# Loading a kernel's mode weights in rows of 4 KB instead of 2 KB, with 64-row products in place of 128-row ones

## The chip, the cores and the metric

The kernel runs on one core of a Trainium2 chip. The metric is the device time of one execution in microseconds (us), the median of several runs. An engine's name stands for the unit that it drives: PE is the matrix unit (TensorE), PEld its weight loads, DVE the vector engine, ACT the scalar engine, POOL GpSimd, SP the sync engine, which only issues transfers here. A DMA is a transfer between the chip's main memory (HBM) and the on-chip memory (SBUF); 16 DMA engines carry all of a core's transfers. PSUM is the memory that PE writes its sums to, in banks of 2 KB per partition.

## What is computed

The first half is a linear attention per batch `b` and head `h` (8 x 8 of them, 576 positions, 64 numbers per head); its result, with the heads side by side, is `x` of 8 x 576 x 512. The second half mixes in frequency space:

```python
X = np.fft.rfft(x, axis=1)                      # along the 576 positions
Xr, Xi = np.real(X[:, :64]), np.imag(X[:, :64]) # 64 modes are kept
Yr = einsum('bmd,mde->bme', Xr, w_r) - einsum('bmd,mde->bme', Xi, w_i)
Yi = einsum('bmd,mde->bme', Xr, w_i) + einsum('bmd,mde->bme', Xi, w_r)
Y[:, :64] = Yr + 1j * Yi
u = x + np.fft.irfft(Y, n=576, axis=1)
out = u + np.maximum(u @ w_ch, 0.0)
```

Every mode `m` has two 512 x 512 matrices of its own, `w_r[m]` and `w_i[m]`, in float32. That is 2 x 64 x 512 x 512 x 4 bytes = 134 MB, and the profile counts 164 MB read from HBM in all. Each weight is used with only 8 batches.

## The kernel before

**Attention.** The Python loop over `n` runs 34 times. Stage `n` computes attention for one batch and two heads (in the first eight stages: two batches and one head), and overlaps four steps of neighbouring stages: the transposes of stage `n+1`, the features of stage `n`, the sums and quotients of stage `n-1`, and `x_mm` of stage `n-2`. `x_mm` (line 344) multiplies the finished part of `x` (`xs_all`) with cosine and sine columns (`CF4`), that is, it takes the Fourier transform of 128 columns of `x`, and puts the result into `XT`: 128 partitions hold 128 of the 512 columns `d`, and the free dimension holds real and imaginary parts, batches and the 64 modes.

**The mode products.** The contraction over the 512 values of `d` is cut in four quarters of 128, and the 64 modes into groups of 8. So there are 32 groups, k = 0 to 31. `weights(k)` (line 156) issues the DMAs of a group, `wr` and `wi`, on POOL's queue; they read float32 and write bf16. `mode_mm(k)` (line 390) makes the products: PE holds a 32-column piece of `XT` (real and imaginary parts of 8 batches and, beside them, zeros or the negated parts) and streams one mode's 512 columns of weights past it. Four such products lie side by side, at PSUM partitions 32j to 32j+31. `mode_sum(k)` adds the result to `Yacc` on DVE. Groups k = 0 to 7 (the first quarter) have a form of their own: their loads and products are already cut into two halves of 64 partitions (lines 166 and 403). Groups k = 8 to 31 have one DMA per tensor (line 162) and 16 products of 128 rows (line 416): 8 with `wr`, then 8 with `wi`.

Three buffers for each of `wr` and `wi` (`NW = 3`) let two groups' loads lie in the queue ahead of the group in use: the loads of group k+3 are issued when `mode_mm(k)` has freed its buffers.

**Order.** Under `manual_schedule` every engine runs its instructions in the order in which the Python code issues them. In the attention loop `mode_mm` is the last PE work of a stage, at most one group per stage, and 22 groups (k = 0 to 21) are done there; groups 8 to 21 fall to the stages n = 17 to 30. The last ten, k = 22 to 31, come in a tail after the loop. There each group is followed on PE by a share of the other work (`pieces`: transposes of `x`, `flip_x`, line 654, and products with `w_ch`, `times_w`, line 665; `reordered`, line 692; for k >= 24 transposes of the sums, line 805, and for every other one `by_batch`, lines 705 and 711). After k = 31 come the inverse transform and the output: lines 753 to 776 on PE, ACT and DVE, and the output DMAs on SP.

Of the kernel before, what the change touches and what calls it, by code (L numbers as in the profile page):

```python
# [21 lines left out]
NCH = 5  # L22
# [4 lines left out]
def kernel(  # L27
# [11 lines left out]
    nc = tc.nc  # L39
# [14 lines left out]
    xs_all = pers.tile([128, B_ * NCH, DMODEL], BF16, name="xs_all")  # L54
# [8 lines left out]
    CF4 = const.tile([128, NCH, 4, 64], BF16, name="CF4")  # L63
# [92 lines left out]
    def weights(k):  # L156
        g, gi = groups[k]
        wt = {}
        for ri, w in ((0, moe_w_r), (1, moe_w_i)):
            t = pw.tile([128, 8, DMODEL], BF16, name=f"w{'ri'[ri]}", tag=f"w{ri}")  # L160
            if gi >= 0:
                nc.gpsimd.dma_start(  # L162
                    t, w[8 * gi:8 * gi + 8, g * 128:(g + 1) * 128, :].rearrange("m p e -> p m e"))
            else:
                for x in range(2):
                    mx = 16 * (-1 - gi) + 8 * x
                    nc.gpsimd.dma_start(
                        t[64 * x:64 * x + 64],
                        w[mx:mx + 8, g * 64:(g + 1) * 64, :].rearrange("m p e -> p m e"))
            wt[ri] = t  # L170
        W[k] = wt
# [172 lines left out]
    def x_mm(st):  # L344
        psx = psum.tile([128, 2, 4, 64], F32, name="psx", tag="tx", bufs=1)
        XT = XTs[st["xt"]][:, 16:80, :].rearrange("p (x y b) m -> p x y b m", x=2, y=4)
        if "bs" in st:

            h = st["h"]
            for i, b in enumerate(st["bs"]):  # L350
                for c in range(NCH):
                    for x in range(2):
                        nc.tensor.matmul(
                            psx[64 * x:64 * x + 64, i, :, :],
                            lhsT=xs_all[:, b * NCH + c, h * 64:(h + 1) * 64],
                            rhs=CF4[:, c, :, :],
                            start=(c == 0), stop=(c == NCH - 1),
                        )
        else:
            g = st["g"]  # L360
            for c in range(NCH):
                nc.tensor.matmul(
                    psx[:, 0, :, :],
                    lhsT=xs_all[:, st["b"] * NCH + c, g * 128:(g + 1) * 128],
                    rhs=CF4[:, c, :, :],
                    start=(c == 0), stop=(c == NCH - 1),
                )
        for i, b in enumerate(st["bs"] if "bs" in st else (st["b"],)):
            nc.scalar.copy(
                XT[:, :, 0:2, b, :],  # L370
                psx[:, i, :, :].rearrange("d (x y) m -> d x y m", x=2),
            )
# [17 lines left out]
    def mode_mm(k, tag="yr"):  # L390
        g, gi = groups[k]
        XT = XTs[1 - g if k < 8 else g % 2]
        wt = W.pop(k)
        if gi < 0:
            psY = psum.tile([128, 2, DMODEL], F32, name="psY2", tag="pC", bufs=1)
            for par in range(2):
                for ri in range(2):
                    for j in range(4):
                        for x in range(2):
                            r = slice(64 * x, 64 * x + 64)  # L400
                            m = 16 * (-1 - gi) + 8 * x + 2 * j + par
                            c0 = (16, 0, 48, 32)[2 * ri + par]
                            nc.tensor.matmul(
                                psY[32 * j:32 * j + 32, x, :],
                                lhsT=XT[r, c0:c0 + 32, m],
                                rhs=wt[ri][r, 2 * j + par, :],
                                start=(par == 0 and ri == 0), stop=(par == 1 and ri == 1),
                            )
            return psY
        psY = psum.tile([128, DMODEL], F32, name="psY", tag=tag, bufs=1)  # L410
        for ri in range(2):
            for par in range(2):
                for j in range(4):
                    m = 8 * gi + 2 * j + par
                    c0 = (16, 0, 48, 32)[2 * ri + par]
                    nc.tensor.matmul(  # L416
                        psY[32 * j:32 * j + 32, :],
                        lhsT=XT[:, c0:c0 + 32, m],
                        rhs=wt[ri][:, 2 * j + par, :],
                        start=(par == 0 and ri == 0), stop=(par == 1 and ri == 1),  # L420
                    )
        return psY

    def mode_sum(k, psY, pb=None):
# [100 lines left out]
    psY = None  # L525
# [3 lines left out]
    with tc.manual_schedule():  # L529
# [18 lines left out]
        for t in qk2s[2]:  # L548
            nc.gpsimd.memset(t[:, :, 9, :], 0.0)
        load_qk(2)  # L550
        weights(0)
        k_in = 1
        transp(S[0], "q")
        transp(S[0], "k")
        for n in range(N + 2):
# [9 lines left out]
            if psY is not None:  # L565
                mode_sum(k_out, psY)
                psY = None
# [17 lines left out]
            while k_in < min(k_out + NW, 2 if n < 3 else 32):  # L585
                weights(k_in)
                k_in += 1
# [17 lines left out]
            if old:  # L605
                x_mm(old)
            e = n - (N + 2 - N_EARLY)
# [14 lines left out]
            if k_out < K_IN_ATTN and n >= after[k_out] + 2:  # L622
                psY = mode_mm(k_out)
# [161 lines left out]
    with tc.manual_schedule():  # L785
        plan = {22: 3, 23: 3, 24: 2, 25: 2, 26: 2, 27: 1, 28: 2, 29: 1, 30: 1, 31: 0}
        while k_out < 32:
            k = k_out
            gi = groups[k][1]
            while k_in < min(k_out + NW, 32):  # L790
                weights(k_in)
                k_in += 1
            if k == 31:
                add_xw(u0)
            yst = mode_sum(k, mode_mm(k, "T3"), pb)
            k_out += 1
            if yst is not None:
# [89 lines left out]
```

## Time and profile before

| | |
|---|---|
| runs | 456.17 us median of 3 (455.78 to 456.91) |
| profiled execution: span | 456.7 us (one core; its span is the time that the profile gives for it) |
| its mean granted PE clock | 0.883 |
| busy share of the span | PE 66%, DVE 64%, ACT 57%, POOL 44%, PEld 43% |
| read from HBM | 163.64 MB |
| moved by DMA, counted as written | 97.70 MB in 84417 packets, of which 77136 have under 2 KB |
| loads of groups 8 to 31 | 24 x 2 DMAs of 1024 KB (as written, bf16), landing 25.8 us (`wr`) and 29.4 us (`wi`) after issue |
| loads of groups 0 to 7 | 8 x 4 DMAs of 512 KB |

Bytes are counted as they are written to SBUF. A weight is read as four bytes and written as two, so a rate of 207 GB/s of weights is 414 GB/s read. The share of the DMA engines can go above 1, as the times of packets overlap. A line of the timeline gives the start in us, the duration from the first instruction's start to the last one's end, the engine, the line of the kernel, the operation, its output and inputs, and how many there are; in brackets is the time for which the engine sat idle before, and who ended it.

### The profile page before, as it was taken

To read this page: it belongs to the slowest core of one execution; us is meant where nothing else is said; L and a number is where in the kernel's file an instruction comes from. 1 tells how busy PE (TensorE), PEld (TensorE's weight loads), DVE (VectorE), ACT (ScalarE), POOL (GpSimd) and SP (SyncE) were. 2 spreads that over 40 slices of the span, in tenths; PEclk is the share of its full clock that TensorE was granted. 3 is DMA by queue.
4 is the path that set the end of the run, shared out by engine and by line. 5 is a ranking of instruction groups with operands and counts; after the bars stand their busy time and mean duration, and the time that the engine had idled before them with its cause. 6 is when DMAs were issued, how large, how long until landed. Compare 5 with 4: busy or idle time off the path is not lost.

```text
span 456.7 us, 11065 instructions
## 1 busy us (share of the span) xinstructions
PE 301.7 (66%) x4637; PEld 197.6 (43%) x4637; DVE 292.0 (64%) x418; ACT 261.8 (57%) x528; POOL 198.8 (44%) x251
## 2 busy tenths in 40 slices
PE   3476776833767677655555544755578878868993
PEld 2355565622555565544333432433344445433341
DVE  6578789844988779876666472776322273653873
ACT  4576887833686877865545452765334455644662
POOL 3956476445563256553435231443021212100993
PEclk9976899876886769998778595999999999998997
DMA  6999999999999999999999999999999999990697
GB/s 179 195 228 222 225 213 226 221 206 216 221 228 217 230 219 222 224 219 229 218 207 217 218 218 218 207 203 207 207 207 207 207 207 207 207 179 11 223 341 299
DMA packets 84417, 97.70 MB, mean 214 GB/s; under 512 B 3152, under 2 KB 77136, under 8 KB 84368
## 3 DMA queue, kind: packets, MB, share of 16 engines
q0 software_dynamic: 75728, 76.75, 101.1%
q1 hardware_dynamic: 8480, 20.19, 12.8%
q8 instruction: 36, 0.59, 0.5%
q14 instruction: 13, 0.11, 0.1%
q10 hardware_dynamic: 160, 0.07, 0.1%
HBM read 163.64 MB, written 9.44 MB: 379 GB/s over the span
## 4 chain that ended last, share of the span: by engine, by line
DMA 34%; issue 24%; DVE 17%; PE 11%; POOL 7%; ACT 3%; SPq 1%; DVEq 0%; POOLq 0%; ACTq 0%
DMA wi<-in_moe_w_i_dram 29%; DVE mkq L233 6%; DMA wr<-in_moe_w_r_dram 4%; DVE xs_all L336 2%; DVE nd L322 2%; DVE tB L315 2%; POOL vaug L270 2%; PE ptr L184 1%; PE psNB L305 1%; ACT AA L240 1%; PE kvz L286 1%; PE psB L753 1%; DVE of L776 1%; SPq L122 1%; POOL wr L162 1%
## 5 line engine op out<-in xcount | busy, mean ns | idle before, releaser
L270 POOL TENSOR_TENSOR vaug<-vn,ee 128x576 bf16<-128x576 f32 x64 | 72.7, 1155 | 63.3 <-ACT ee L255 50.2
L240 ACT ACTIVATE AA<-psT 128x1024 bf16<-128x1024 f32 x64 | 62.0, 1021 | 43.6 <-PE psT L208 43.1
L262 ACT ACTIVATE e<-mkq 64x4 f32<-64x4 f32 (+1 forms) x128 | 26.3, 206 | 61.5 <-DVE mkq L233 59.2
L244 ACT ACTIVATE AA<-psk 128x1024 bf16<-128x1024 f32 x64 | 61.4, 1010 | 0.0
L162 POOL DMA_DIRECT2D wr<-in_moe_w_r_dram x24 | 21.9, 912 | 86.6 <-PE psY L416 77.8
L416 PEld LDWEIGHTS <-XT 128*32 128x32 bf16 x384 | 17.1, 171 | 56.6 <-issue 46.4
L667 ACT CAST xw<-psW 128x1024 bf16<-128x1024 f32 x17 | 17.2, 1013 | 40.5 <-PE psW L665 34.6
L233 DVE TENSOR_REDUCE mkq<-psk 128x8 f32<-128x1024 f32 x32 | 38.8, 1213 | 0.7 <-PE psk L199 0.7
L233 DVE TENSOR_REDUCE mkq<-psq 128x8 f32<-128x1024 f32 x32 | 38.9, 1217 | 0.4 <-PE psq L199 0.4
L435 DVE TENSOR_TENSOR Yacc<-psY,Yacc 128x512 f32<-128x512 f32 x16 | 11.0, 689 | 42.5 <-PE psY L416 42.5
L416 PE MATMUL psY<-wi,XT 128*32 128x512 bf16 x192 | 18.0, 435 | 28.8 <-DMA wi<-in_moe_w_i_dram 28.8
L286 PE MATMUL kvz<-vaug,AA 64*128 64x65 bf16 x1152 | 29.2, 210 | 11.5 <-POOL vaug L275 9.8
L190 DVE COPY kT<-ptr 128x640 bf16<-128x640 bf16 x32 | 15.7, 492 | 32.5 <-PE ptr L184 32.5
L665 PE MATMUL psW<-wchb,sT 128*128 128x512 bf16 x136 | 33.5, 391 | 2.1 <-ACT xw L667 2.1
L315 DVE TENSOR_TENSOR tB<-psNB,e 128x650 f32<-128x650 f32 x32 | 26.7, 833 | 11.2 <-PE psNB L305 10.6
L305 PEld LDWEIGHTS <-AA 128*128 128x128 bf16 x640 | 29.0, 110 | 9.3 <-issue 8.9
L286 PEld LDWEIGHTS <-AA 64*128 64x128 bf16 x1152 | 25.1, 107 | 15.9 <-issue 11.8
L162 POOL DMA_DIRECT2D wi<-in_moe_w_i_dram x24 | 21.1, 880 | 23.8 <-PE psY L416 20.5
L322 DVE TENSOR_TENSOR nd<-psNA,tB 128x650 f32<-128x650 f32 x32 | 26.7, 835 | 4.1 <-DVE tB L315 0.5
L416 PE MATMUL psY<-wr,XT 128*32 128x512 bf16 x192 | 17.0, 424 | 18.0 <-DMA wr<-in_moe_w_r_dram 8.7
L336 DVE TENSOR_TENSOR xs_all<-nd,rden 128x640 bf16<-128x640 f32 x32 | 28.0, 874 | 1.1
L184 PE MATMUL ptr<-ident_b,k 128*128 128x128 bf16 x160 | 17.9, 257 | 14.8 <-DVE qT L190 12.6
(132 smaller groups left out, 705.4 us busy)
## 6 DMA issues: line engine op xcount, KB each, us to landing
wr<-in_moe_w_r_dram POOLq DMA_DIRECT2D x24, 1024.0 KB, 25.8
wi<-in_moe_w_i_dram POOLq DMA_DIRECT2D x24, 1024.0 KB, 29.4
wr<-in_moe_w_r_dram POOLq DMA_DIRECT2D x16, 512.0 KB, 15.9
wi<-in_moe_w_i_dram POOLq DMA_DIRECT2D x16, 512.0 KB, 19.6
out_dram<-of SPq DMA_DIRECT2D x16, 512.0 KB, 3.8
vn<-in_v_dram SPq DMA_DIRECT2D x24, 288.0 KB, 5.8
q<-in_q_dram POOLq DMA_DIRECT2D x12, 288.0 KB, 19.3
k<-in_k_dram POOLq DMA_DIRECT2D x12, 288.0 KB, 20.0
```

The source lines that it names most:

```text
L162: nc.gpsimd.dma_start(t, w[8 * gi:8 * gi + 8, g * 128:(g + 1) * 128, :].rearrange("m p e -> p m e"))
L233: nc.vector.tensor_reduce(out=o, in_=i, axis=AX.X, op=ALU.max, apply_absolute_value=True)
L240: nc.scalar.activation(AA[:, 0, ab, 0:1024].rearrange("f (x j p) -> f j x p", j=2, p=64), st["psT"].rearrange("f j (x p) -> f j x p", p=64 ...
L244: nc.scalar.activation(AA[:, 1, ab, 0:1024].rearrange("p (c j f) -> p j c f", c=4, j=2), st["psk"], ACT.Exp, scale=sc)
L270: nc.gpsimd.tensor_tensor(out=vaug[:, ab, :, 0:64], in0=st["v"], in1=ee[:, ab, :].unsqueeze(2).to_broadcast([128, 9, D_]), op=ALU.mult,)
L286: nc.tensor.matmul(kvz[:, hh, ab * 65:(ab + 1) * 65], lhsT=AA[r, 1, ab, 128 * j:128 * j + 128], rhs=vaug[r, ab, j, :], start=(j == 0), sto ...
L305: nc.tensor.matmul(p[:, hh, 65 * c:65 * c + 65], lhsT=AA[:, 0, ab, x:x + 128], rhs=kvzF[:, hh, ab * 65:(ab + 1) * 65], start=True, stop=True,)
L315: nc.vector.tensor_tensor(out=tB, in0=st["psNB"], in1=e2.unsqueeze(3).to_broadcast([128, 2, NCH, 65]), op=ALU.mult,)
L322: nc.vector.tensor_tensor(out=nd, in0=st["psNA"], in1=st["tB"], op=ALU.add)
L336: nc.vector.tensor_tensor(out=xo, in0=nd[:, :, :, 0:64], in1=rden.to_broadcast([128, 2, NCH, 64]), op=ALU.mult,)
L416: nc.tensor.matmul(psY[32 * j:32 * j + 32, :], lhsT=XT[:, c0:c0 + 32, m], rhs=wt[ri][:, 2 * j + par, :], start=(par == 0 and ri == 0), sto ...
L665: nc.tensor.matmul(ps[:, x, :], lhsT=sT[:, x, dc, :], rhs=wchb[:, dc, :], start=(dc == 0), stop=(dc == 3))
```

## The change

Groups 8 to 31 are loaded in another layout. Partition p of each half (64 partitions) takes two neighbouring rows of `w`, d = 2p and 2p+1 of the quarter, which lie behind one another in HBM: one row of 2 x 512 x 4 = 4096 bytes is read and 2048 written, where it was 2048 and 1024. The lower half of the partitions holds the group's first four modes, the upper half the other four. One DMA per tensor becomes two, each of 64 partitions x 4 modes x 1024 elements (128 x 8 x 512 before).

`XT` has to follow: its partitions 0 to 63 now hold the even or the odd `d` (chosen by `i`, in the free dimension) for the lower four modes of each group, and 64 to 127 those for the upper four. `x_mm` makes it with 20 products of 128 x 64 by 128 columns, where it had 5 of 128 x 128 by 256. `mode_mm` has 32 products of 64 rows per group where it had 16 of 128: twice over `i`, each with half of the contraction.

```diff
@@ weights
-                nc.gpsimd.dma_start(
-                    t, w[8 * gi:8 * gi + 8, g * 128:(g + 1) * 128, :].rearrange("m p e -> p m e"))
+                for x in range(2):
+                    mx = 8 * gi + 4 * x
+                    nc.gpsimd.dma_start(
+                        t[64 * x:64 * x + 64].rearrange("p (m i) e -> p m (i e)", i=2),
+                        w[mx:mx + 4, g * 128:(g + 1) * 128, :].rearrange(
+                            "m (p i) e -> p m (i e)", i=2))
@@ x_mm
-            for c in range(NCH):
-                nc.tensor.matmul(
-                    psx[:, 0, :, :],
-                    lhsT=xs_all[:, st["b"] * NCH + c, g * 128:(g + 1) * 128],
-                    rhs=CF4[:, c, :, :],
-                    start=(c == 0), stop=(c == NCH - 1),
-                )
+            for i in range(2):
+                for c in range(NCH):
+                    cf = CF4[:, c].rearrange("p y (q r) -> p (y q) r", r=4)
+                    for x in range(2):
+                        nc.tensor.matmul(
+                            psx[64 * x:64 * x + 64, 0, :, 32 * i:32 * i + 32],
+                            lhsT=xs_all[:, st["b"] * NCH + c, g * 128 + i:(g + 1) * 128:2],
+                            rhs=cf[:, x::2, :],
+                            start=(c == 0), stop=(c == NCH - 1),
+                        )
@@ mode_mm
-                for j in range(4):
-                    m = 8 * gi + 2 * j + par
-                    c0 = (16, 0, 48, 32)[2 * ri + par]
-                    nc.tensor.matmul(
-                        psY[32 * j:32 * j + 32, :],
-                        lhsT=XT[:, c0:c0 + 32, m],
-                        rhs=wt[ri][:, 2 * j + par, :],
-                        start=(par == 0 and ri == 0), stop=(par == 1 and ri == 1),
-                    )
+                for i in range(2):
+                    for j in (0, 2, 1, 3):
+                        r = slice(64 * (j // 2), 64 * (j // 2) + 64)
+                        m = 2 * (j % 2) + par
+                        c0 = (16, 0, 48, 32)[2 * ri + par]
+                        nc.tensor.matmul(
+                            psY[32 * j:32 * j + 32, :],
+                            lhsT=XT[r, c0:c0 + 32, 32 * i + 4 * gi + m],
+                            rhs=wt[ri][r, 2 * m + i, :],
+                            start=(ri == 0 and par == 0 and i == 0),
+                            stop=(ri == 1 and par == 1 and i == 1),
+                        )
```

## The prediction

> **What bounds the kernel now.** I read the forty slices of the page first.
>
> ```profile
> PEclk9976899876886769998778595999999999998997
> DMA  6999999999999999999999999999999999990697
> GB/s 179 195 228 222 225 213 226 221 206 216 221 228 217 230 219 222 224 219 229 218 207 217 218 218 218 207 203 207 207 207 207 207 207 207 207 179 11 223 341 299
> ```
>
> The DMA engines are full from the second slice to about 407 us, where the last weights run out. Wherever weights alone move, the rate is 207 GB/s (414 read), so a group of 4.19 MB costs 4.19 MB / 414 GB/s = 10.13 us. That looks like a kernel bound by its loads. The timeline of PE says that only a part of it is. In the attention stages PE stands waiting for `wi`, up to the last group done there, k = 21:
>
> ```profile
> 280.93 1.11 PE L416 MATMUL psY<-wi,XT 128*32 128x512 bf16 x8 [4.77 <-DMA wi<-in_moe_w_i_dram]
> ...
> 291.29 0.69 PE L416 MATMUL psY<-wi,XT 128*32 128x512 bf16 x8 [0.20 <-DMA wi<-in_moe_w_i_dram]
> ...
> 312.08 0.69 PE L416 MATMUL psY<-wi,XT 128*32 128x512 bf16 x8 [0.97 <-DMA wi<-in_moe_w_i_dram]
> ```
>
> The waits of PE between 165 and 335 us add up to 37.1 us for the two tensors:
>
> ```profile
> PE psY L416 <- DMA wi<-in_moe_w_i_dram: 28.4, 11, 5.2
> ...
> PE psY L416 <- DMA wr<-in_moe_w_r_dram: 8.7, 3, 4.1
> ```
>
> In the tail (k = 22 to 31) the picture turns. From 331 to 403 us no product waits for a DMA: PE goes from group to group with its own work between, and short waits for DVE and ACT. The loads only catch it at k = 30, for 1.16 us. The last `wi` was issued at 388.4 and landed 26.0 us later, at 414.4; PE came to it at 415.56.
>
> ```profile
> 331.07 0.69 PE L416 MATMUL psY<-wr,XT 128*32 128x512 bf16 x8 [0.67 <-ACT xw L388]
> 331.50 0.69 PE L416 MATMUL psY<-wi,XT 128*32 128x512 bf16 x8
> ...
> 402.78 0.69 PE L416 MATMUL psY<-wr,XT 128*32 128x512 bf16 x8 [0.78 <-DVE sT L657]
> 404.63 0.69 PE L416 MATMUL psY<-wi,XT 128*32 128x512 bf16 x8 [1.16 <-DMA wi<-in_moe_w_i_dram]
> ...
> 410.72 3.22 PE L665 MATMUL psW<-wchb,sT 128*128 128x512 bf16 x8
> ...
> 415.56 0.69 PE L416 MATMUL psY<-wr,XT 128*32 128x512 bf16 x8
> ```
>
> So a faster load is worth something up to 312 us, and after 331 us every added us of PE work is paid in full. The change gives the one and takes the other.
>
> **The loads.** Per group 1024 rows of 4 KB replace 2048 of 2 KB. No row of the trace has 4 KB reads with a cast, so the gain is bounded by rows next to it. The rows of q and k are read in 2304 bytes with the same cast, an eighth longer; around their landings (176.7 and 179.6 us) the rate is 208 in place of 207:
>
> ```profile
> 36.00:40.00 4.00, 1.88 (x54) 1.53 (x54) 3.52 (x7) 3.52 (x10) 1.19 (x3) 0.88 1.24 206
> 176.00:180.00 4.00, 3.01 (x57) 2.27 (x55) 3.46 (x6) 2.77 (x7) 3.87 (x6) 1.00 1.24 208
> 340.00:360.00 20.00, 16.60 (x132) 8.68 (x134) 5.26 (x8) 9.50 (x10) 3.50 (x4) 1.00 1.24 207
> ```
>
> (Window, its length, PE, PEld, DVE, ACT and POOL busy, PE clock, DMA share, GB/s.) If a row costs a fixed part and a part by bytes, 0.5% at an eighth longer means a fixed part of 0.5% / 0.111 = 4.5%, and rows twice as long save half of it: 2.25%, 0.23 us per group. With rounding it may be 0 to 1%, so 0 to 0.45 us per group; I take 0.23. The Trainium skill (DMA: Bandwidth & Descriptors, "Why small descriptors are slow (HBM only)") gives a packet 3 cycles beside its 32-byte beats; estimated from that, 2 x (64 + 3) = 134 cycles become 131, 2.2%, and the sum would be the same.
>
> Halves of 64 partitions cost nothing by the window 36 to 40 us: the first quarter's loads have that form and run at 206. POOL issues four DMAs per group instead of two. A 1024-row one takes 0.90 us, a 512-row one 0.71; in line with these a 256-row one would take 0.6, so 2.4 us instead of 1.8 per group. Behind it on POOL stands `vaug` (line 270), which waits 2 to 2.6 us for ACT in these stages anyway; if that cover were gone, 0.6 us per stage would go to a stage that waits 2.7 us for its weights on average.
>
> The gain starts at k = 11: k = 8 to 10 are loaded ahead and wait for their stages, and their buffers come free when PE gets there (170.7 us), as now. The queue is then just short of empty (share 1.18 instead of 1.20 for such a mix between 172 and 176 us), and buffers freed later than now cost it 0.4 us (the added `wr` products, below). So `wi` of k = 18 lands 8 x 0.23 - 0.4 = 1.4 us earlier, that of k = 21 2.1.
>
> **The products.** The trace has both forms.
>
> ```profile
> L416 PE MATMUL psY<-wi,XT 128*32 128x512 bf16 x192 | 18.0, 435 | 28.8 <-DMA wi<-in_moe_w_i_dram 28.8
> L403 PE MATMUL psY<-wr,XT 64*32 64x512 bf16 x128 | 7.9, 443 | 1.9 <-ACT XT L369 1.8
> ```
>
> ```profile
> 67.26 0.48 PE L403 MATMUL psY<-wr,XT 64*32 64x512 bf16 x8
> 67.47 0.48 PE L403 MATMUL psY<-wi,XT 64*32 64x512 bf16 x8
> ```
>
> Of the 128-row form 8 take 0.43 us, start to start (331.07 to 331.50): four lie side by side, two rounds of 0.215. Of the 64-row form 8 take 0.21 (67.26 to 67.47): eight lie side by side in one such round. A round is thus the passing of 512 columns, whatever the rows. The changed `mode_mm` uses only four places (two quarters of the columns in the lower rows, the other two in the upper), each eight times per group: 8 rounds where there are 4. That is 0.86 us more per group, 0.43 before `wi` and 0.43 behind its landing. Bounds: 0 (eight side by side) to 32 products one by one (last but one rival).
>
> **`x_mm`.** Five products of 256 columns take 0.63 us now; 20 of 128 columns, two side by side, are 10 passes of 0.053 = 0.53 us, and the nearest row with 64 columns of weights and 128 streamed (line 181) starts ten in 0.31, so 20 in 0.62. The other end is line 353, 20 of 256 columns in 1.2 us: 0.6 more. I take 0. Until n = 31 it has cover either way (DVE's 2.7 us of lines 315 to 336, or ACT); only in the last two stages would 0.6 each be seen.
>
> **The sum**, on the profiled execution (456.7 us). k = 18: `wi` at 280.93 - 1.4 = 279.5, its products 0.43 longer. k = 19: `wr` at 290.40 - 1.0 = 289.4, `wi` 0.86 behind it, at 290.3 (landing 289.6). k = 20: 299.4 and 300.3. k = 21: 309.2 and 310.0, which is also its landing: 2.1 earlier than 312.08. k = 22: 331.07 - 2.1 + 0.43 = 329.4. Eight groups (22 to 29) add 8 x 0.86 = 6.9: k = 30 at 408.0, `wi` at 408.9 without a wait, 4.2 later than 404.63. With the rest of its products +4.65, and k = 31 adds 0.86: +5.5, so 462.2 us. The loads (last one about 410) no longer matter there. The slow products at 410.72 (3.22 us at a clock of 0.52, where others take 1.9) are left as they are; without them it would be 1.4 less. The runs' median is 0.5 below this execution: **461.7 us**.
>
> **The rivals.**
> - *Rows of 4 KB are no faster*, per byte as now: k = 22 comes 0.8 later, the end 8.0: 464.2. For it speaks that 207 against 208 is within rounding.
> - *They are twice as good* (0.45 per group): k = 18 lands 3.2 earlier, but the stages from k = 19 on then bind themselves; k = 22 comes 3.45 earlier, the end is +3.75: 459.9. More speed of the loads hardly shows any more.
> - *Faster than before: the 64-row products overlap as at line 403.* If the extra rounds vanish in overlap, `mode_mm` costs what it costs now, k = 22 comes 2.1 earlier, k = 30 loses its wait, and the end comes 3.5 earlier: 452.7. It decides below some 0.3 us added per group. Against it: line 403 has eight places, this code four.
> - *Row halves shut each other out.* The order of j alternates lower and upper rows, and all write one PSUM bank; in line 403 the halves write two banks. If products of different halves can't run together, 32 x 0.213 = 6.8 us replace 1.7 of each group: 10 x 6 us in the tail and 14 x 6 less the 37 us of waits before, about 560 us. The Trainium skill (TensorEngine Tiling (Array Packing), "Gotcha 1: PSUM Pressure") says that different row tiles can't access one bank at the same time; by that rule this case would be the likely one, and no row here has it. Against it: the halves write different partitions.
> - *Loads in halves are slower.* The first ones ran at 173 to 185 GB/s between 18 and 22 us. At 180 a group would take 11.6 us, and 21 groups add 31 us: 488. Against it: 206 at 36 to 40 us and after.
>
> **How the numbers follow.** Forecast 0.66 (its own range 460 to 463.5: the slow clock, 0.1 us more or less per group); no gain of the loads 0.12; twice the gain 0.08; overlap 0.07; one bank 0.04; slow halves 0.03. What a measurement of this kernel can tell is about 0.3%, 1.4 us. Faster by more: 0.07 for the overlap and 0.01 for the unforeseen; within: 0.06, from parts of overlap and gain together; slower: 0.86. The range leaves out overlap, bank and slow halves: 457.5 to 466.
>
> **What would show it.** PE's `wr` and `wi` in the tail 0.86 us apart, twice 0.43; tail loads at 212 GB/s; `wi` of k = 21 started near 310, k = 22 near 329; no DMA wait at k = 30. Products 0.43 apart, or the tail's groups no longer spaced (the ten from 331 to 415 us) by 0.9 more, would make it wrong; so would waits for `wi` in the tail.

## The result, and the profile after

The changed kernel takes 475.36 us (median of 4 runs, 472.45 to 476.93) against 456.22 us (4 runs) on the same chip: a ratio of 1.040, 95% interval 1.036 to 1.044. It is slower, as forecast, but by 19 us and not by 5.5, and lies 9 us above the range. The profiled execution has a span of 474.2 us, where the working of the prediction ends at 462.2.

The slices of the page of after, to be laid beside the first fence of the prediction:

```profile
PEclk9985998867785888997979789998599999999998
DMA  6999999999999996999999999999999999950597
GB/s 178 192 228 227 217 227 218 218 217 217 214 225 210 231 173 126 231 221 220 221 217 225 211 231 222 211 211 211 204 162 189 184 201 205 211 110 1 188 345 298
DMA packets 60616, 97.80 MB, mean 206 GB/s; under 512 B 3921, under 2 KB 28753, under 8 KB 60561
```

Where weights alone move and nothing holds them up, the rate is now 211 GB/s, where it was 207, and the packets under 2 KB have fallen from 77136 to 28753: the rows are longer and move faster, as worked out. But there are holes that before does not have: 173 and 126 GB/s in slices 15 and 16 (166 to 190 us), and 162 to 205 from 344 us on. The second hole is harmless: there the loads wait for buffers that PE has not yet emptied. The first one is a loss in the middle of the loads. In windows of 4 us (columns as in the prediction's table of windows):

```profile
168.00:172.00 4.00, 2.27 (x56) 1.83 (x56) 2.86 (x6) 3.44 (x9) 3.18 (x5) 1.00 0.84 143
172.00:176.00 4.00, 2.50 (x56) 1.96 (x56) 3.22 (x6) 2.66 (x7) 0.61 (x1) 0.80 0.99 187
176.00:180.00 4.00, 3.58 (x56) 2.86 (x59) 2.88 (x5) 3.31 (x9) 2.46 (x3) 0.50 0.29 49
180.00:184.00 4.00, 3.74 (x75) 1.91 (x65) 2.98 (x4) 1.96 (x6) 2.37 (x4) 0.84 0.52 89
184.00:188.00 4.00, 2.77 (x85) 2.54 (x81) 3.30 (x8) 3.98 (x9) 2.77 (x5) 1.00 1.06 193
```

The mode products in the timeline of PE of after (the bracketed waits for DMA that before shows at these groups are gone):

```profile
179.38 1.93 PE L425 MATMUL psY<-wr,XT 64*32 64x512 bf16 x16
...
316.55 1.09 PE L425 MATMUL psY<-wr,XT 64*32 64x512 bf16 x16
317.47 1.03 PE L425 MATMUL psY<-wi,XT 64*32 64x512 bf16 x16
342.93 1.94 PE L425 MATMUL psY<-wr,XT 64*32 64x512 bf16 x16 [0.67 <-ACT xw L395]
...
421.48 1.09 PE L425 MATMUL psY<-wr,XT 64*32 64x512 bf16 x16 [0.78 <-DVE sT L667]
422.34 1.09 PE L425 MATMUL psY<-wi,XT 64*32 64x512 bf16 x16
...
432.33 1.09 PE L425 MATMUL psY<-wr,XT 64*32 64x512 bf16 x16
```

The tail is near the prediction. From k = 23 on `wr` and `wi` start 0.86 to 0.92 us apart, the wait for `wi` at k = 30 (422.34) is gone, and from k = 22 to k = 30 it takes 78.55 us, 6.84 more than the 71.71 of before; 6.9 was predicted (how much of that agreement is chance is said further down). What is wrong lies ahead of it: k = 22 starts at 342.93, not at 329.4. Group k = 8 is already late: it starts at 179.38, and at 170.72 in before. By the working of the prediction neither the longer rows nor the slower products count before k = 11.

The waits tell what PE stood for. The rows of after, by engine and line, with the total in us, how often, and the longest:

```profile
POOL wr L164 <- PE psY L425: 64.2, 9, 14.9
...
PE kvz L290 <- POOL vaug L279: 50.6, 17, 7.7
...
POOL wr L164 <- DMA wi<-in_moe_w_i_dram: 23.5, 12, 2.7
POOL wi L164 <- DMA wi<-in_moe_w_i_dram: 12.1, 7, 2.4
POOL wi L164 <- DMA k<-in_k_dram: 11.7, 5, 3.0
POOL wi L164 <- DMA wr<-in_moe_w_r_dram: 10.3, 6, 2.1
```

The same row of before is "PE kvz L286 <- POOL vaug L275: 9.8, 2, 6.1". `kvz` (`kv_mm`, line 290) is PE's first product with `vaug`, the scaled values that POOL makes (`vscale`, lines 274 and 279). So PE's 37 us of waits for weights have been exchanged for 51 us of waits for POOL (its waits for `wi` at line 425 are down to 3.7 us), and POOL itself stands before its *DMA issues*, waiting for the landing of other DMAs. All rows of line 164 that a DMA ended add up to 67.7 us in 39 waits; the loads of groups 8 to 31 in before (line 162) have one such wait, of 3.1 us.

POOL's own timeline of after shows by which rule it waits:

```profile
110.13 0.76 POOL L143 DMA_DIRECT2D q<-in_q_dram  x1 [0.19 <-issue]
111.77 0.70 POOL L143 DMA_DIRECT2D k<-in_k_dram  x1 [0.88 <-DMA wr<-in_moe_w_r_dram]
115.16 0.64 POOL L164 DMA_DIRECT2D wr<-in_moe_w_r_dram  x1 [2.68 <-DMA wi<-in_moe_w_i_dram]
118.20 0.61 POOL L164 DMA_DIRECT2D wr<-in_moe_w_r_dram  x1 [2.40 <-DMA wi<-in_moe_w_i_dram]
120.54 0.61 POOL L164 DMA_DIRECT2D wi<-in_moe_w_i_dram  x1 [1.73 <-PE psk L203]
122.84 0.61 POOL L164 DMA_DIRECT2D wi<-in_moe_w_i_dram  x1 [1.69 <-DMA wr<-in_moe_w_r_dram]
123.47 2.27 POOL L274 TENSOR_TENSOR vaug<-vn,ee 128x576 bf16<-128x576 f32 x2
125.68 0.26 POOL L279 CAST vaug<-ee 128x18 bf16<-128x18 f32 x1
125.81 0.66 POOL L164 DMA_DIRECT2D wr<-in_moe_w_r_dram  x1
127.94 0.61 POOL L164 DMA_DIRECT2D wr<-in_moe_w_r_dram  x1 [1.47 <-DMA wi<-in_moe_w_i_dram]
129.63 0.61 POOL L164 DMA_DIRECT2D wi<-in_moe_w_i_dram  x1 [1.07 <-DMA q<-in_q_dram]
132.87 0.61 POOL L164 DMA_DIRECT2D wi<-in_moe_w_i_dram  x1 [2.63 <-DMA k<-in_k_dram]
```

Count the DMAs. The `wi` at 129.63 waited for a `q`: the `q` of 110.13 is the eighth DMA before it. The `wi` at 132.87 waited for `k`: the `k` of 111.77 is the eighth before. The records of the DMAs in the traces name the semaphore that each one signals: in both kernels POOL's DMAs take eight of them in turn (110 to 117), and in neither does a DMA of POOL start before the eighth before it has landed. So no more than eight of POOL's DMAs are on their way, whatever their size, and the ninth holds POOL, with all that stands behind it in POOL's order. With two DMAs per group, three groups in flight make six, and a `q` and a `k` fill the eight. With four per group, three groups make twelve. From then on POOL issues at the rate of landings, 2 to 3 us apart; the four issues of a stage take 8 to 10 us with their waits, and `vaug`, which comes behind them, is late:

```profile
147.69 0.61 POOL L164 DMA_DIRECT2D wi<-in_moe_w_i_dram  x1 [1.63 <-DMA wr<-in_moe_w_r_dram]
148.32 2.27 POOL L274 TENSOR_TENSOR vaug<-vn,ee 128x576 bf16<-128x576 f32 x2
```

```profile
150.83 1.17 PE L290 MATMUL kvz<-vaug,AA 64*128 64x65 bf16 x36 [7.73 <-POOL vaug L279]
```

The first of these is POOL's, the second PE's timeline of after. PE stands for 7.7 us here for a load that has nothing to do with its stage. The same product in PE's timeline of before:

```profile
141.32 1.10 PE L286 MATMUL kvz<-vaug,AA 64*128 64x65 bf16 x36
```

There POOL issued the stage's two loads at 131.27 and 132.36 and started this `vaug` at 135.26, and PE did not wait for it. After is 9.5 us behind at this point, and 8.7 are left when k = 8 starts.

The hole at 168 to 188 us follows from that: all three buffers are full until k = 8 frees one.

### The profile page after: what moved, and what is told of

The parts are those of the page before. It is cut to its first block, busy times and chain, and to the rows that moved or that the text cites. A ratio compares the mean times of both kernels' runs of the same rounds, so it can differ in the third digit from the quotient of the medians.

```text
span 474.2 us, 12581 instructions
## 1 busy us (share of the span) xinstructions
PE 322.7 (68%) x5362; PEld 218.9 (46%) x5381; DVE 294.0 (62%) x418; ACT 262.3 (55%) x528; POOL 214.4 (45%) x299
## 2 busy tenths in 40 slices
DMA packets 60616, 97.80 MB, mean 206 GB/s; under 512 B 3921, under 2 KB 28753, under 8 KB 60561
## 4 chain that ended last, share of the span: by engine, by line
PE 29%; DMA 29%; DVE 13%; ACT 9%; POOL 9%; issue 8%; SPq 1%; DVEq 0%; ACTq 0%; POOLq 0%
DMA wi<-in_moe_w_i_dram 16%; DMA q<-in_q_dram 7%; PE psW L675 6%; PE psY L425 6%; DMA wr<-in_moe_w_r_dram 5%; POOL vaug L274 4%; DVE mkq L237 3%; ACT AA L244 2%; DVE nd L326 2%; DVE xs_all L340 2%; POOL wi L164 2%; PE kvz L290 2%; ACT AA L248 2%; PE psx L369 2%; PE pt L664 1%
## 5 line engine op out<-in xcount | busy, mean ns | idle before, releaser
L164 POOL DMA_DIRECT2D wr<-in_moe_w_r_dram x48 | 30.1, 630 | 96.9 <-PE psY L425 64.2
L290 PE MATMUL kvz<-vaug,AA 64*128 64x65 bf16 x1152 | 28.6, 208 | 51.4 <-POOL vaug L279 50.6
L164 POOL DMA_DIRECT2D wi<-in_moe_w_i_dram x48 | 29.6, 624 | 56.3 <-DMA wi<-in_moe_w_i_dram 12.1
L290 PEld LDWEIGHTS <-AA 64*128 64x128 bf16 x1152 | 25.7, 105 | 55.4 <-issue 50.6
L425 PEld LDWEIGHTS <-XT 64*32 64x32 bf16 x768 | 31.2, 138 | 28.6 <-issue 20.8
L299 ACT CAST kvzF<-kvz 128x260 bf16<-128x260 f32 x32 | 12.1, 379 | 44.3 <-PE kvz L290 44.1
L425 PE MATMUL psY<-wr,XT 64*32 64x512 bf16 x384 | 28.7, 418 | 8.2 <-ACT AA L252 4.1
L309 PEld LDWEIGHTS <-AA 128*128 128x128 bf16 x640 | 30.3, 112 | 6.8 <-issue 6.3
L675 PE MATMUL psW<-wchb,sT 128*128 128x512 bf16 x126 | 31.3, 379 | 2.6 <-ACT xw L677 2.1
L425 PE MATMUL psY<-wi,XT 64*32 64x512 bf16 x384 | 27.3, 381 | 3.7 <-DMA wi<-in_moe_w_i_dram 3.7
```

Source lines behind the costliest of these rows:

```text
L164: nc.gpsimd.dma_start(t[64 * x:64 * x + 64].rearrange("p (m i) e -> p m (i e)", i=2), w[mx:mx + 4, g * 128:(g + 1) * 128, :].rearrange("m ...
L290: nc.tensor.matmul(kvz[:, hh, ab * 65:(ab + 1) * 65], lhsT=AA[r, 1, ab, 128 * j:128 * j + 128], rhs=vaug[r, ab, j, :], start=(j == 0), sto ...
L309: nc.tensor.matmul(p[:, hh, 65 * c:65 * c + 65], lhsT=AA[:, 0, ab, x:x + 128], rhs=kvzF[:, hh, ab * 65:(ab + 1) * 65], start=True, stop=True,)
L425: nc.tensor.matmul(psY[32 * j:32 * j + 32, :], lhsT=XT[r, c0:c0 + 32, 32 * i + 4 * gi + m], rhs=wt[ri][r, 2 * m + i, :], start=(ri == 0 an ...
L675: nc.tensor.matmul(ps[:, x, :], lhsT=sT[:, x, dc, :], rhs=wchb[:, dc, :], start=(dc == 0), stop=(dc == 3))
```

## The experiments

Theory Q: the number of POOL's DMAs in flight. Rival P: the slower products themselves delay the attention stages. Rival H: transfers to halves of the partitions are slower. Each run is compared with the kernel before on the same chip: 456.20 us (13 runs) for the first four, 456.16 us (8 runs) for the next four, 457.10 us (17 runs) for the last. In the table, "k = 22" is the start of that group's first product in the profiled execution, "tail" the time from there to the first product of k = 31, "kvz" PE's wait there for `vaug`.

| kernel | median us | ratio [95%] | span | k = 22 | tail | kvz |
|---|---|---|---|---|---|---|
| before | 456.2 | 1 | 456.7 | 331.07 | 84.5 | 9.8 |
| after | 475.36 | 1.040 [1.036, 1.044] | 474.2 | 342.93 | 89.4 | 50.6 |
| e1_split_only | 467.61 | 1.027 [1.024, 1.029] | 467.0 | 344.24 | 81.7 | 48.1 |
| e2_products_twice | 466.21 | 1.022 [1.018, 1.027] | 461.3 | 330.78 | 88.7 | 9.9 |
| e3_rows_only | 453.37 | 0.993 [0.991, 0.996] | 452.7 | 329.94 | 81.7 | 10.7 |
| e4_after_vaug_first | 471.61 | 1.035 [1.030, 1.040] | 471.0 | 340.77 | 88.4 | 7.4 |
| e6_after_one_dma | 463.91 | 1.019 [1.015, 1.023] | 459.1 | 328.88 | 88.4 | 10.4 |
| e7_split_by_modes | 470.34 | 1.031 [1.026, 1.035] | 466.9 | 343.24 | 82.6 | 47.8 |
| e5_before_vaug_first | 463.52 | 1.015 [1.011, 1.020] | 463.3 | 337.82 | 84.4 | 4.0 |
| e8_after_two_ahead | 477.24 | 1.045 [1.040, 1.049] | 477.2 | 346.98 | 88.4 | 3.8 |
| e9_parts_in_halves | 455.51 | 0.996 [0.994, 0.998] | 455.0 | 332.31 | 81.8 | 8.4 |

### Only the number of DMAs: e1_split_only

```diff
@@ before, weights
-                nc.gpsimd.dma_start(
-                    t, w[8 * gi:8 * gi + 8, g * 128:(g + 1) * 128, :].rearrange("m p e -> p m e"))
+                for x in range(2):
+                    d0 = g * 128 + 64 * x
+                    nc.gpsimd.dma_start(
+                        t[64 * x:64 * x + 64],
+                        w[8 * gi:8 * gi + 8, d0:d0 + 64, :].rearrange("m p e -> p m e"))
```

> The kernel before, with each load of groups 8 to 31 cut into two DMAs of 64 partitions; rows stay 2 KB, products and layout as before. Theory Q (queue): the program gives POOL's DMAs eight semaphores in turn, so the ninth DMA outstanding waits, on POOL, for the first to land; with four DMAs per group instead of two POOL stands still, vaug behind it comes late and so does PE. Then this kernel shows most of the surprise: k = 22 starts 9 to 14 us later than the 331 us of before, total 465 to 470 us, and PE waits 40 us or more for vaug (9.8 before). Rival P (products): the delay in the attention stages comes from the 64-row products and the new x_mm; then this kernel is within 2 us of 456. Rival H (halves): 64-partition transfers are slower; then the rate in the tail is below 200 GB/s instead of 207.

467.61 us. Products, rows and `x_mm` are those of before, and yet k = 8 starts at 180.60 and k = 22 at 344.24, even a little later than in after. The waits of PE and of POOL in e1_split_only:

```profile
PE kvz L289 <- POOL vaug L278: 48.1, 14, 9.0
```

```profile
POOL wi L164 <- DMA wr<-in_moe_w_r_dram: 17.0, 9, 2.2
POOL wi L164 <- DMA wi<-in_moe_w_i_dram: 14.8, 7, 3.1
POOL wr L164 <- DMA wi<-in_moe_w_i_dram: 14.7, 9, 2.4
```

That is the picture of after. The rate between 320 and 330 us is 206 GB/s, where before has 207, so halves of 64 partitions are not slow: H falls. The delay comes without the slower products, so P is not needed for it. Q stands. The extra issue time alone is too small: an issue takes 0.70 us here, so four of them take 1.0 us more per group than the two of before, and single waits of `kvz` reach 9.0 us.

### Only the products: e2_products_twice

The products of `mode_mm` (k from 8 on) are made twice and both added, 32 of 128 rows in place of 16, in 8 rounds as in after (the mode part of the output is doubled). The loads are those of before.

```diff
@@ before, mode_mm
-            for par in range(2):
-                for j in range(4):
+            for rep in range(2):
+                for par in range(2):
+                    for j in range(4):
...
-                        start=(par == 0 and ri == 0), stop=(par == 1 and ri == 1),
+                            start=(rep == 0 and par == 0 and ri == 0),
+                            stop=(rep == 1 and par == 1 and ri == 1),
```

> The kernel before, with all mode products of groups 8 to 31 made and added twice (16 more products per group, four side by side, so 0.86 us more per group as in the changed kernel; the mode part of the output is doubled). Loads as before. Theory Q: the attention stages hardly move (k = 22 at 331 to 332.5), the ten groups of the tail add about 7 us, total 461 to 465. Rival P: the attention stages lose 10 us or more here too, total 470 or above.

466.21 us, 1.2 us above what was expected, with a profiled execution at the low end of its runs (463.12 us, span 461.3). In that one, k = 22 stands where it stood (330.78), `kvz` waits 9.9 us, and the tail takes 88.7 us in place of 84.5. The tail of before contains the wait at k = 30 and the slow products at 410.72; the tails of e1 and e3 have neither and take 81.7 us, so the products cost the tail 7.0 us. They cost the attention nothing in this execution; P falls for the attention as far as it shows. The other three runs are 2.5 to 4.4 us slower, and no profile of them says where.

### Only the rows: e3_rows_only

One DMA per tensor as in before, 128 partitions with rows of 4 KB. The partitions then hold 256 rows of four modes and not 128 of eight, so the products multiply other weights than the reference's; their shapes and number are those of before.

```diff
@@ before, weights
-                    t, w[8 * gi:8 * gi + 8, g * 128:(g + 1) * 128, :].rearrange("m p e -> p m e"))
+                    t.rearrange("p (m i) e -> p m (i e)", i=2),
+                    w[8 * gi:8 * gi + 4, (g - 1) * 128:(g + 1) * 128, :].rearrange(
+                        "m (p i) e -> p m (i e)", i=2))
```

> The kernel before, with each load of groups 8 to 31 still one DMA of 128 partitions but in 512 rows of 4 KB (four modes of 256 rows; the products get other weights than they should). Products as before. Theory Q and the prediction: 212 GB/s in place of 207, k = 22 2 us earlier, the end 2 to 3.5 us earlier: 452.5 to 454.5. If the gain of 4 KB rows in the changed kernel was an artefact of its emptier queue, 207 GB/s and 456.

453.37 us, 0.66% faster, span 452.7. The prediction's "overlap" rival gave a median of 452.7 for faster loads without slower products. The rate is 212 GB/s.

### After, with vaug ahead of the loads: e4_after_vaug_first

```diff
@@ after, the loop over n
-            if n < 4:
+            if cur:
                 vscale(cur)
...
-            if cur and n >= 4:
-                vscale(cur)
```

> The changed kernel, with the making of vaug put ahead of the weights' loads on POOL's queue in every stage. Theory Q: PE's wait for vaug goes from 50.6 to under 15 us and most of the surprise comes back: 462 to 467 us. If the waits for the queue hurt by starving the loads and not through vaug, or if P holds, it stays at 473 to 477.

471.61 us, only 4 us back, where 8 to 13 were expected. The wait of `kvz` is gone as wanted (7.4 us). But the loads now stand behind `vaug`, and `vaug` behind ACT; the first line is from the waits of POOL, the second from the page of e4:

```profile
POOL vaug L274 <- ACT ee L259: 66.2, 19, 6.3
```

```profile
GB/s 180 195 229 215 221 121 220 217 218 217 218 220 222 224 228 136 216 221 221 221 223 220 223 220 221 212 212 211 210 211 212 204 201 207 210 114 1 189 346 301
```

There are two holes. In the first (121 GB/s, 59 to 71 us) a `wr` that after issues at 60.51 is issued at 69.14, behind a `vaug` that waits 4.1 us for ACT. In the second (136 GB/s, 177 to 188 us) k = 8 is still late (177.52), and the loads that it makes room for then stand behind another wait for ACT, of 4.3 us. So it is not the order alone. As I read it, with eight places of half the size POOL has to be at hand at every landing, and it can't be while it also waits for ACT; no run separates that from the late start of k = 8. My expectation had left it out.

### Before, with vaug ahead: e5_before_vaug_first

The same edit in the kernel before, as a control.

> The kernel before with vaug ahead of the weight loads on POOL in every stage, the control to the same edit of after (which gave back some 4 of 19 us and moved the hold from vaug to the loads, whose issue then stood behind vaug's wait for ACT). Theory Q: with two DMAs per group there is little to gain (kvz waits 9.8 us for vaug in all) and the loads come up to 3 us later per group, though the depth of three groups covers that: 454 to 460, vaug's wait of kvz 2 to 8 us. A theory by which the order on POOL is the whole cost of the change would have a gain here of the 10 us that kvz waits: 446 to 450.

463.52 us, 7 us slower; both expectations missed. With two DMAs per group the loads first, `vaug` second is the better order by these 7 us. The timeline of PE, ACT and POOL shows why a late load feeds itself (the fences are one for each engine):

```profile
210.26 1.10 PE L416 MATMUL psY<-wi,XT 128*32 128x512 bf16 x8 [5.18 <-DMA wi<-in_moe_w_i_dram]
211.69 0.64 PE L208 MATMUL psT<-qT,w 64*128 64x512 bf16 x2
```

```profile
212.43 1.94 ACT L240 ACTIVATE AA<-psT 128x1024 bf16<-128x1024 f32 x2 [6.03 <-PE psT L208]
214.92 0.21 ACT L255 ACTIVATE ee<-mkq 128x9 f32<-128x9 f32 x1
```

```profile
215.22 2.27 POOL L270 TENSOR_TENSOR vaug<-vn,ee 128x576 bf16<-128x576 f32 x2 [8.54 <-ACT ee L255]
217.43 0.25 POOL L275 CAST vaug<-ee 128x18 bf16<-128x18 f32 x1
217.57 0.94 POOL L162 DMA_DIRECT2D wr<-in_moe_w_r_dram  x1
```

PE waits 5.2 us for a `wi`; the stage's `psT` stands behind it on PE, ACT behind `psT`, `vaug` behind ACT, and the next load behind `vaug`: it is issued at 217.57, 7 us after the products that freed a buffer began.

### After, with one DMA per tensor: e6_after_one_dma

Everything of after but the count of DMAs: `x_mm` with 20 products, 32 products of 64 rows per group, rows of 4 KB, and one DMA of 128 partitions per tensor as in e3 (so the weights are again other ones than the reference's).

```diff
@@ after, weights
-                for x in range(2):
-                    mx = 8 * gi + 4 * x
-                    nc.gpsimd.dma_start(
-                        t[64 * x:64 * x + 64].rearrange("p (m i) e -> p m (i e)", i=2),
-                        w[mx:mx + 4, g * 128:(g + 1) * 128, :].rearrange(
-                            "m (p i) e -> p m (i e)", i=2))
+                nc.gpsimd.dma_start(
+                    t.rearrange("p (m i) e -> p m (i e)", i=2),
+                    w[8 * gi:8 * gi + 4, (g - 1) * 128:(g + 1) * 128, :].rearrange(
+                        "m (p i) e -> p m (i e)", i=2))
```

> The kernel after with its two DMAs per tensor and group made one again: 128 partitions, four modes, 4 KB rows, the same 1 MB (the partitions then hold 256 rows of four modes, not 128 rows of eight, so the products multiply other weights; their number, order and shapes are those of after). So the 4 KB rows, the 64-row products and the new x_mm stay; only the number of DMAs goes back to two per group. Theory Q (POOL's DMAs take turns at eight places, and four per group do not fit): the delay in attention goes, k = 22 back at 329 to 332, PE's waits of kvz for vaug back to 9 to 15 us, no dip of the rate at 176 to 188, the tail stays that of after or of the doubled products (86 to 90 us), in all 458 to 466. Rival P (the slower products themselves delay attention): 470 to 476. Rival H (halves of 64 partitions are slow to move): it would also predict a gain, but the kernel that only split the loads moved its halves at 206 GB/s against 207, so H has little left.

463.91 us, where 461.7 was predicted for after. PE's timeline in e6 has k = 22 at the predicted place (329.4):

```profile
328.88 1.09 PE L423 MATMUL psY<-wr,XT 64*32 64x512 bf16 x16 [0.67 <-ACT xw L393]
329.74 1.09 PE L423 MATMUL psY<-wi,XT 64*32 64x512 bf16 x16
```

and PE's waits for `vaug` are back at the size of before:

```profile
PE kvz L288 <- POOL vaug L277: 10.4, 3, 6.4
```

The loss of after now splits in two, by medians: 463.91 - 456.16 = 7.8 us for rows, products and `x_mm` together, and 475.36 - 463.91 = 11.4 us for two DMAs more per group. The second part alone, in e1, was 467.61 - 456.20 = 11.4 us. That the two agree so closely is partly chance: the four runs of e6 lie between 460.93 and 466.69, and by the profiled executions alone the split is 2.4 and 15.1 us.

### The other cut: e7_split_by_modes

```diff
@@ before, weights
-                nc.gpsimd.dma_start(
-                    t, w[8 * gi:8 * gi + 8, g * 128:(g + 1) * 128, :].rearrange("m p e -> p m e"))
+                for x in range(2):
+                    mx = 8 * gi + 4 * x
+                    nc.gpsimd.dma_start(
+                        t[:, 4 * x:4 * x + 4, :],
+                        w[mx:mx + 4, g * 128:(g + 1) * 128, :].rearrange("m p e -> p m e"))
```

> The kernel before, with each weight load of k from 8 on cut in two by modes: two DMAs of 128 partitions, four modes each, 2 KB rows (the other cut, by partitions, took 467.6). Theory Q: it is the number of DMAs that counts, not which partitions they go to: 464 to 470, k = 22 at 341 to 347, waits of kvz for vaug 40 to 55 us. Rival H (halves of 64 partitions, or the two transfers' sharing of ports): as before, 455 to 458, waits of kvz for vaug at 10 us.

470.34 us and 47.8 us of `kvz` waits, with all 128 partitions in every DMA. It is the count, not the halves. The loss is 14.2 us, where e1 lost 11.4; why this cut costs 2.8 us more stays open.

### Fewer ahead: e8_after_two_ahead

```diff
@@ after
-    NW = 3
+    NW = 2
```

> The kernel after with two groups of weights ahead in place of three (eight DMAs in place of twelve, less those of q and k). Theory Q: POOL stands before fewer loads and kvz's waits for vaug fall from 50.6 to 15 to 35 us, but with a group less in flight the queue runs empty more often (some 5 us per third of the attention's groups), so that the total is no better than after: 472 to 485. If the depth is not needed at all, the waits go and the time is that of the prediction, 460 to 465.

477.24 us (475.38 to 483.31). The waits of `kvz` fall to 3.8 us, further than expected, and the time is no better: the depth is needed. PE waits for `wi` again, 20.4 us at line 425 and 17.1 at line 410, and the rate shows holes of 114 and 140 GB/s.

### A version that beats both: e9_parts_in_halves

What would keep the long rows without either loss? Two DMAs per group and 128-row products. A DMA of all eight modes' row pairs fills 64 partitions; so `w_r` goes to the lower and `w_i` to the upper half of one tile of 16 KB per partition, and `XT` gets the spectrum's columns for `w_r` below and those for `w_i` above. One product of 128 rows then sums both parts, 16 per group as in before.

```diff
@@ after, weights
+        both = pw.tile([128, 16, DMODEL], BF16, name="w", tag="w")
         for ri, w in ((0, moe_w_r), (1, moe_w_i)):
...
+                nc.gpsimd.dma_start(
+                    both[64 * ri:64 * ri + 64].rearrange("p (m i) e -> p m (i e)", i=2),
+                    w[8 * gi:8 * gi + 8, g * 128:(g + 1) * 128, :].rearrange(
+                        "m (p i) e -> p m (i e)", i=2))
@@ after, x_mm
-                            psx[64 * x:64 * x + 64, 0, :, 32 * i:32 * i + 32],
+                            psx[64 * x:64 * x + 64, 0, 2 * i:2 * i + 2, :],
...
-                            rhs=cf[:, x::2, :],
+                            rhs=CF4[:, c, 2 * x:2 * x + 2, :],
@@ after, mode_mm
+        for i in range(2):
+            for par in range(2):
+                for j in range(4):
+                    m = 2 * j + par
+                    c0 = (16, 0, 48, 32)[2 * i + par]
+                    nc.tensor.matmul(
+                        psY[32 * j:32 * j + 32, :],
+                        lhsT=XT[:, c0:c0 + 32, 8 * gi + m],
+                        rhs=wt[:, 2 * m + i, :],
+                        start=(par == 0 and i == 0), stop=(par == 1 and i == 1),
+                    )
```

> A version meant to beat both kernels, with the result of the reference. For k from 8 on, one DMA moves all eight modes of w_r as 4 KB rows into partitions 0 to 63, a second one those of w_i into partitions 64 to 127 of the same tile: two DMAs per group as in before, rows as in after. x_mm (20 products, as in after) lays the spectrum for w_r in the lower and the one for w_i in the upper half of the partitions, so that one product of 128 rows sums both parts: 16 products of 128 rows per group, as in before. Theory Q (after's loss is the count of DMAs plus the 64-row products): both losses are gone and the gain of the rows stays: 452 to 456 (452.7 to 453.4 by the kernel that changed the rows alone; up to 1 us more because all 16 products now wait for the second DMA, where eight went ahead before), k = 22 at 328 to 332, rate 211 to 213, waits of kvz for vaug 9 to 12 us. Rival H (64 partitions per DMA are slower once two of them are not in flight side by side): a rate under 205 and 460 or more.

455.51 us (12 runs) against 457.10: 0.996 [0.994, 0.998], faster than both kernels, and 0.4% where the rows alone gave 0.66%. The rate is 212 GB/s and the tail 81.8 us. The rest is in the attention: k = 22 starts at 332.31 (e3: 329.94), 2.4 us later, where I had allowed 1 us. I put it down to the products of a group, none of which can start before its second DMA has landed. The waits for it:

```profile
PE psY L421 <- DMA w<-in_moe_w_i_dram: 27.7, 5, 7.9
```

Two more waits, of 3.7 and 3.5 us, are put down to ACT in that view, but the products begin 0.13 to 0.14 us after a landing of `w_i` (216.56 after 216.42, 266.25 after 266.12), as in most of the five. Together that is 34.9 us, against 29.9 us of waits for weights in e3 between 165 and 333 us. It fits, but `x_mm` differs from that of e3 too. The waits of `kvz` are 8.4 us.

## Why the prediction was wrong

**The loads: right.** 212 GB/s was predicted from 4.5% of fixed cost per row. After and e6 show 211 to 212, and in e3 k = 21 starts 1.9 us earlier (308.48 for 310.42), where 2.1 was predicted for its landing. That halves of 64 partitions cost nothing was right too (206 in e1, and e7 with whole partitions loses no less).

**The products: right.** 0.43 us more for each tensor was predicted; `wr` to `wi` is 0.86 to 0.92 in after from k = 23 on, 0.43 to 0.52 in before. That eight groups of the tail took 6.84 us more, where 6.9 was predicted, is partly luck: 1.0 us of it lies at k = 22, where PE's granted clock was 0.68 (342.9 to 346.3 us). In e6, where the same products had a clock of 1.00, the eight groups add 5.81 us: six of them 0.83 to 0.84, the groups k = 26 and 28 only 0.40. So the rival that the products overlap is out, and so is the one that row halves shut each other out: products of both halves write one bank here and take 0.054 us each (0.86 / 16), not 0.213. The sentence of the Trainium skill cited there (TensorEngine Tiling (Array Packing), "Gotcha 1: PSUM Pressure") does not hold for this case, where the halves write different partitions.

**`x_mm`: right.** 20 products are 0.77 to 0.79 us long where five were 0.71.

**The tail: right but for two small terms.** The wait at k = 30 is gone as said. The slow products at 410.72 (3.22 us) have no counterpart (1.89 us at 428.82), which the prediction priced at 1.4 us less. With it, its tail of 90.8 us (329.4 to 420.2) is 89.4, and 89.4 was measured. The agreement to a tenth is chance: the 1.1 us that the eight groups fell short of 6.9 were made up by the 1.0 us of slow clock at k = 22. The tails of e4, e6 and e8, with the same products, take 88.4.

**The step that failed** is POOL's: "POOL issues four DMAs per group instead of two. ... so 2.4 us instead of 1.8 per group. Behind it on POOL stands `vaug` (line 270), which waits 2 to 2.6 us for ACT in these stages anyway". The issue itself was right: 0.61 to 0.64 us each. What it left out is that POOL must wait before it may issue, so that four issues take 8 to 10 us of POOL and not 2.4. The uncovered end that it named, "0.6 us per stage", was no bound. The trace of before held the clue, in the waits of POOL. Its loads of the first quarter (line 167), which already go four to a group, and the loads of `k` beside them waited for DMAs that have nothing to do with them:

```profile
POOL k L143 <- DMA wi<-in_moe_w_i_dram: 7.0, 2, 4.2
POOL wr L167 <- DMA wi<-in_moe_w_i_dram: 6.0, 3, 3.1
POOL wi L167 <- DMA k<-in_k_dram: 4.2, 2, 2.8
```

The prediction does not mention them. In place of 329.4, k = 22 came at 342.93, 13.5 us late. Less 1.4 us for the slow products this leaves 12.1, and 474.2 - 462.2 = 12.0 had to be explained. And e6, which has the whole change but those two DMAs, has k = 22 at 328.88. Its span is 459.1 us, 3.1 less than the working's 462.2: 1.4 for the slow products, 1.1 for the eight groups and 0.5 at k = 22.

**Its start at k = 11** fell with it: the delay begins in stages ahead of k = 8, when POOL issues the four DMAs each of k = 8, 9 and 10 (115 to 148 us). "Just short of empty" was wrong for the queue as well: k = 8 was 8.7 us late, and the queue ran down to 49 GB/s.

**Still open.** Of the 11.9 us by which k = 22 lags before, 8.7 are there at k = 8, and 6.5 come between k = 21 and k = 22 (25.5 us from `wi` to `wr`, 19.0 in before; the groups between had made up some). In that last stretch PE's granted clock was 0.57 between 330 and 340 us, where before has 1.00, beside waits of `kvz` of 3.5 us. (e1 and e7, with four DMAs per group as well, have 0.50 and 0.57 there.) How much of it is the clock and how much the late `vaug` was not told apart. Nor was it shown where the other runs of e2 and e6 lose 2 to 6 us against their profiled executions, which were the fastest of each.

## What to carry to other kernels

Count the transfers that an engine has on their way, not only the bytes and the time to issue them: here the ninth DMA from POOL waits, on POOL, for the landing of the first, and everything behind it in POOL's order waits too. Where a trace shows a DMA issue waiting for the landing of an unrelated DMA, as here, look for such a limit: once it is reached, cutting a transfer in two halves the bytes that can be on their way. If a layout needs halves of the partitions, fill each half with another tensor, so that the number of transfers and the rows of the products stay as they were.

## What the runs showed of the hardware

- Rows of 4 KB read with a cast move at 211 to 212 GB/s as written, rows of 2 KB at 206 to 207, a gain of 2.4%, whether the transfer fills 128 partitions (e3) or 64 (after, e9).
- A POOL issue takes 0.63 us on average for 256 rows of 4 KB (after), 0.70 for 512 rows in 64 partitions (e1 with 2 KB, e9 with 4 KB), 0.76 for 512 rows in 128 partitions (e3 with 4 KB, e7 with 2 KB), and 0.90 for 1024 rows of 2 KB (before): a quarter of the rows takes more than two thirds of the time.
- Sixteen 64 x 32 products with 512 columns, alternating between the halves of the rows, four at a time, take 0.86 us; eight with 128 rows take 0.43, so a round of four costs the same 0.215 with half of the rows.
